# Start addresses of the SBUF slots in a fused attention and two-layer feed-forward kernel

## Chip, cores, metric

One core of a Trainium2 chip. The metric is the device time of one execution in microseconds (us). The kernel before takes 512.0 us, the median of three runs (511.82 to 512.19).

## What is computed

```python
scores = softmax(causal(q @ k.T / sqrt(64)))       # 2 batches x 12 heads, 448 tokens, head size 64
x = (scores @ v), heads side by side               # 896 tokens x 768
h = x @ w_in1;  x = (h * cos(h)) @ w_out1          # 768 -> 2048 -> 768
h = x @ w_in2
g = where(h >= 1, h, where(h <= -1, 0, (h + 1)**2 / 4))
out = g @ w_out2                                   # 2048 -> 768
```

The weights arrive as 64-bit floats.

## The kernel before

**Stages.** Attention comes first. Its last matmuls give way to ten groups of six products (`FILL`, line 599) of the first feed-forward layer. Then come the rest of that layer (`stage_in_plain`, line 854), its output layer (`stage_out(0)`, line 1009), the second input layer (`stage_in_split`, lines 1274 and 1369) and the second output layer (`stage_out(1)`, line 1009 again). The layers use two-level Strassen-like sums, so that one product serves several blocks.

**The matmuls that matter here.** From line 599 to the end TensorE runs 2106 matmuls of one shape: a 128x128 block of weights against 128x448 elements of the token side, both `fp32r` (4 bytes). Every value is split in a high and a low part, so each block product is three matmuls: weight high times token high, weight high times token low, weight low times token high. Each matmul is preceded by its own load of the weights (`LDWEIGHTS`), and the load for the next matmul runs while the current one streams its tokens.

**Slots.** Weights lie in four slots, `w0` to `w3`, each 128 partitions x 6144 bytes, used in rotation (`sw` in `stage_out` takes `w{t % 4}`). Token-side operands lie in slots of 7168 bytes: `x0` to `x5` hold the attention's output, then in `stage_out` the split halves `sx` (a ring of `x0`, `x1`, `x2`), then in the second input layer the pieces `rx` (slots `x0` to `x9`, `x14`) and `re` (slot `e0`) by the table `PIECES`. The first product of `stage_out(0)` is an exception: its token side `sx0.0h`, `sx0.0l` lies in `b0` and `b1`. The slots `b0` to `b6` hold raw 64-bit rows as 16-bit words (`RAW` = 3076 of them), later also sums and results.

**Addresses.** `place` gives each slot its tile. The slots in `EARLY` come from pool `x_p`, which is open from the start; all others come from `sum_p`, which is opened over the attention's pools once those are done. Slots follow each other in the order in which they are first asked for. 6152 bytes of a raw slot take up 6176, which is 24 x 256 + 32, so each raw slot moves all that follow it by 32 bytes modulo 256. A weight block (512 bytes), a half of a weight slot (3072) and the 1792 bytes of 448 tokens are whole multiples of 256, so within a slot every operand begins at the slot's own remainder.

**Order.** `Plan` sets the order of the work from line 854 on by modelled durations and fixed due times; `STEPS` sets it by hand for the attention. Neither looks at addresses.

Of the kernel before, what the change touches and what calls it, by code (L numbers as in the profile page):

```python
# [12 lines left out]
F32 = mybir.dt.float32  # L13
# [10 lines left out]
P = 128  # L24
# [5 lines left out]
U16 = mybir.dt.uint16  # L30
# [251 lines left out]
def attention_then_two_ffn(  # L282
# [23 lines left out]

    UW = KD * P
    RAW = 4 * UW + 4

    const = ctx.enter_context(tc.tile_pool(name="const", bufs=1))  # L310
    x_p = ctx.enter_context(tc.tile_pool(name="x", bufs=1))
# [14 lines left out]
    EARLY = {f"x{c}" for c in range(KD)} | {"b0", "b1", "b2", "w0", "w1", "w2", "w3"}  # L326
    pools = [x_p]

    def place(slot, name, shape, dtype):
        return pools[slot not in EARLY].tile(shape, dtype, tag=slot, name=name)  # L330

    raws, ready = {}, {}

    def fetch_unit(u, raw):
        w_in, f = (w_in1, w_in2)[u // KF], u % KF
        nc.sync.dma_start(
            out=raw[:, 1 : RAW - 3].rearrange("p (n f) -> p n f", f=4 * P),
            in_=w_in[:, f * P : (f + 1) * P].bitcast(U16).rearrange("(n p) f -> p n f", p=P),
        )

    def load_unit(u):
        raws[u] = place(f"b{u % 3}", f"raw{u}", [P, RAW], U16)
        fetch_unit(u, raws[u])
# [28 lines left out]
    def decode_unit(u):  # L372

        raw = raws[u]
        decode_top(tops[0], raw)
        yield
        decode_bits(words(raw), tops[0], raw)
        yield
        fl = words(raw).bitcast(F32)
        ready[u] = w = place(f"w{u}", f"w{u}", [P, 2, UW], F32R)  # L380
        nc.scalar.copy(out=w[:, 0], in_=fl)
        yield
        nc.vector.tensor_tensor(out=w[:, 1], in0=fl, in1=f32(w[:, 0]), op=ALU.subtract)
        load_unit(u + 3)
# [7 lines left out]
    class Pair:  # L392
# [5 lines left out]
        def load(self, _=None):  # L398
            n = self.n
            self.k = ld.tile([P, S], F32, tag="k", name=f"k{n}", bufs=6)  # L400
            nc.sync.dma_start(out=self.k, in_=k[n])
            self.qr = self.q = ld.tile([P, S], F32, tag="qr", name=f"qr{n}")
            (nc.scalar if n == 0 else nc.sync).dma_start(out=self.qr, in_=q[n])
# [174 lines left out]
    def decode(u):  # L578

        if u not in decodes:  # L580
            decodes[u] = decode_unit(u)
        run(decodes[u])
# [3 lines left out]
    def ffn_in_part(u, x, b, chunks):  # L586

        if u not in parts:
            bank = int(next(pairs_of_banks))
            parts[u] = (bank, ready[u], set())  # L590
            made.append(u)
        bank, w, done = parts[u]
        s = slice(b * S, (b + 1) * S)
        for c in chunks:
            first = not any((b, i) in done for i in range(KD))
            done.add((b, c))
            last = all((b, i) in done for i in range(KD))
            for n, (a, t) in enumerate(((0, 0), (0, 1), (1, 0))):
                nc.tensor.matmul(  # L599
                    psum[:, bank + b, :S], w[:, a, c * P : (c + 1) * P], x[c][:, t, s],  # L600
                    start=(first and n == 0), stop=(last and n == 2),
                )
# [11 lines left out]
    def one_bank():  # L614
        return psum[:, int(next(single_banks))]

    with ExitStack() as attn:
        ld = attn.enter_context(tc.tile_pool(name="ld", bufs=4))
        st = attn.enter_context(tc.tile_pool(name="st", bufs=3))
        once = attn.enter_context(tc.tile_pool(name="once", bufs=1))  # L620
        pairs = [Pair(n) for n in range(B * NP)]
        pairs[0].load()

        ones = nc.const_aps.tensor(1.0, [P, 512], BF16)
        warm = one_bank()
        for _ in range(8):
            nc.tensor.matmul(warm, ones[:, :P], ones, start=True, stop=True)
        ident = once.tile([P, P], F32, name="ident")
        make_identity(nc, ident)


        mask32 = once.tile([QB, QB], F32, name="mask32")
        make_causal_mask(nc, mask32, mask_val=MASKED)
        both = once.tile([P, 3 * HALF], BF16, name="both")
        nc.vector.memset(both, 0.0)
        above = once.tile([P, 2, 2, HALF], BF16, name="above")
        nc.vector.memset(above, MASKED)
        for h in (slice(0, HALF), slice(HALF, P)):
            nc.vector.tensor_copy(out=both[h, HALF:QB], in_=ident[h, h])
            for m in range(2):  # L640
                nc.vector.tensor_copy(out=above[h, m, 0], in_=mask32[h, h])
        upper, lower = both[:, HALF:], both[:, HALF:QB]
        for top in tops:
            nc.gpsimd.memset(top, 0)

        nc.scalar.activation(out=once.tile([P, 1], F32, name="first"), in_=half, func=AF.Exp)
        x1 = [place(f"x{c}", f"x1{c}", [P, 2, NT], F32R) for c in range(KD)]
        pairs[1].load()
        for word in STEPS.split():
            what, n = re.fullmatch(r"([A-Za-z]+)(\d+)", word).groups()  # L650
            n = int(n)
            if what == "raw":
                load_unit(n)
            elif what == "D":
                decode(n)
            elif what == "F":
                u, b, chunks = FILL[n]
                ffn_in_part(u, x1, b, chunks)
            elif what[0] == "l":
                (pairs[n].load if what == "l" else pairs[n].load_v)()  # L660
            else:
                getattr(pairs[n], what[0])(what[1:])
# [5 lines left out]
    MW = ML * P  # L668
    sum_p = ctx.enter_context(tc.tile_pool(name="sum", bufs=1))
    pools.append(sum_p)  # L670

    plan = Steps()
    things = {}

    def buf(name, slot, shape, dtype=F32, given=()):
        plan.buf(name, slot, given)
        things[name] = (slot, shape, dtype)

    def tile_of(name):
        t = things[name]  # L680
        if isinstance(t, tuple):
            t = things[name] = place(t[0], name, t[1], t[2])
        return t
# [72 lines left out]
    def load_raw(u, slot):  # L756
        name = f"raw{u}"
        buf(name, slot, [P, RAW], U16)
        load(f"L{u}", lambda: fetch_unit(u, tile_of(name)), [(name, p) for p in RAW_PARTS])
# [38 lines left out]
    def ws_buf(k, j, h):  # L798
        name = f"ws{k}.{j}.{h}"
        if name not in things:  # L800
            buf(name, WS_SLOT[k, h][j], [P, 2, 2, MW])
        return name
# [7 lines left out]
    def rows(k, n):  # L810
# [3 lines left out]
        name = f"rows{k}.{n}"  # L814
        buf(name, ROW_SLOT[k][n], [P, RAW], U16)
        ws = ws_buf(k, j, q // 2)

        def fetch():
            nc.sync.dma_start(out=tile_of(name)[:, 1 : RAW - 3], in_=w_out[f * P : (f + 1) * P, :].bitcast(U16))

# [650 lines left out]
```

## Time and profile before

| what | us |
|---|---|
| median of three runs | 512.0 |
| the profiled execution | 511.94 |
| its span, first to last instruction | 510.2 |
| TensorE busy (share of the span) | 504.0 (99%) |
| VectorE busy | 367.8 (72%) |
| ScalarE busy | 350.3 (69%) |
| GpSimd busy | 103.7 (20%) |

The page's busy time of TensorE counts overlapping matmuls as one stretch, so 99% says that it hardly idles, not how densely its matmuls follow each other. The length of one matmul in the trace (some 0.36 us) is longer than the distance from one start to the next (some 0.20 us), since matmuls are pipelined. The pace is therefore read from starts: of n matmuls that follow each other, from the first start to the next group's first start, divided by n.

### The profile page before, as it was taken

Reading aid. Unit: us, or ns where it says so; the run is one execution under the profiler, and the core shown is the slowest. Engines: PE = TensorE matmul, PEld = TensorE weight load, DVE = VectorE, ACT = ScalarE, POOL = GpSimd, SP = SyncE. Lnnn points to the kernel's source line nnn. Section 1 sums busy time; section 2 is a strip of 40 time slices with the busy share of each in tenths; the row PEclk is TensorE's granted clock in tenths of the full one; section 3 lists DMA queues with packets and bytes.
Section 4 is the critical chain, followed back from the end, with each engine's and each line's share of the span. In section 5 each row is a group of like instructions: output and inputs, shape, how many; then the busy total and the mean of one; then the engine's idle time right before and its main releaser. Section 6 shows DMA issues by size and latency. Waiting matters only on the chain.

```text
span 510.2 us, 7594 instructions
## 1 busy us (share of the span) xinstructions
PE 504.0 (99%) x2810; PEld 448.7 (88%) x2810; DVE 367.8 (72%) x502; ACT 350.3 (69%) x607; POOL 103.7 (20%) x165
## 2 busy tenths in 40 slices
PE   8999999999999999999999999999999999999997
PEld 4766678999999999999999999999999999999996
DVE  7878876587656656687668977777878699764760
ACT  5998977687656556655557778888788678656441
POOL 4847660000000113334001101111101012610000
PEclk9999999999999999999999999999999999999999
DMA  8845124778692478999226786775685869992111
GB/s 272 296 134 174 41 78 159 255 246 255 236 275 71 107 160 187 222 187 191 51 69 174 170 214 184 215 193 154 172 284 129 251 153 276 171 221 52 54 55 55
DMA packets 45861, 87.26 MB, mean 171 GB/s; under 512 B 2816, under 2 KB 33536, under 8 KB 45824
## 3 DMA queue, kind: packets, MB, share of 16 engines
q1 hardware_dynamic: 36464, 61.51, 36.5%
q0 software_dynamic: 9216, 25.04, 27.0%
q8 instruction: 22, 0.36, 0.3%
q10 hardware_dynamic: 144, 0.23, 0.1%
q14 instruction: 15, 0.12, 0.1%
HBM read 58.98 MB, written 2.75 MB: 121 GB/s over the span
## 4 chain that ended last, share of the span: by engine, by line
PE 97%; DVE 1%; DMA 1%; issue 0%; ACT 0%; POOL 0%; POOLq 0%
PE psum L1009 40%; PE psum L854 20%; PE psum L1274 15%; PE psum L1369 6%; PE psum L555 4%; PE psum L529 4%; PE psum L442 4%; PE psum L599 2%; DMA qr<-in_q 1%; PE psum L427 1%; DVE nma L466 0%; PE psum L452 0%; PE psum L455 0%; DVE nmc L466 0%; DVE raw L368 0%
## 5 line engine op out<-in xcount | busy, mean ns | idle before, releaser
L854 PE MATMUL psum<-x,w 128*128 128x448 f32 x516 | 103.7, 363 | 0.0
L854 PEld LDWEIGHTS psum<-x,w 128*128 128x128 f32 x516 | 96.8, 188 | 6.7
L368 DVE SCALAR_TENSOR_TENSOR raw<-raw,top 128x768 uint32<-128x768 uint32 x32 | 30.6, 957 | 14.7 <-ACT top L359 11.5
L359 ACT CAST top<-raw 128x768 f16<-128x768 bf16 x26 | 27.9, 1074 | 9.6 <-DMA raw<-in_moe_w_in 9.5
L529 PE MATMUL psum<-ident,p 128*128 128x128 f32 x192 | 24.8, 278 | 0.6 <-POOL p L509 0.6
L555 PE MATMUL psum<-pT,v 128*64 128x448 f32 (+3 forms) x192 | 23.2, 385 | 0.9 <-ACT pT L546 0.9
L1274 PE MATMUL psum<-rx,w1g 128*128 128x448 f32 x108 | 24.0, 366 | 0.0
L1274 PE MATMUL psum<-rx,w0g 128*128 128x448 f32 x108 | 23.8, 364 | 0.0
L1274 PE MATMUL psum<-rx,w2g 128*128 128x448 f32 x108 | 23.7, 364 | 0.0
L529 PEld LDWEIGHTS psum<-ident,p 128*128 128x128 f32 x192 | 20.6, 141 | 3.3 <-issue 0.9
L555 PEld LDWEIGHTS psum<-pT,v 128*64 128x64 f32 x192 | 12.6, 136 | 12.0 <-issue 6.4
L509 POOL TENSOR_SCALAR p<-p,ra 128x384 f32<-128x384 f32 (+1 forms) x48 | 22.2, 482 | 3.1 <-DVE rb L494 1.2
L707 POOL DMA_DIRECT2D raw<-raw x12 | 10.2, 850 | 61.1 <-DVE raw L712 48.3
L509 POOL TENSOR_SCALAR p<-p,rb 128x256 f32<-128x256 f32 (+1 forms) x32 | 18.2, 581 | 19.1 <-DVE rb L495 18.0
L1274 PEld LDWEIGHTS psum<-rx,w1g 128*128 128x128 f32 x108 | 20.3, 188 | 1.8
L1274 PEld LDWEIGHTS psum<-rx,w2g 128*128 128x128 f32 x108 | 20.3, 188 | 1.5
L1274 PEld LDWEIGHTS psum<-rx,w0g 128*128 128x128 f32 x108 | 20.3, 188 | 1.5
L442 PE MATMUL psum<-k,q 64*128 64x256 f32 (+2 forms) x132 | 20.5, 409 | 0.0
L442 PEld LDWEIGHTS psum<-k,q 64*128 64x128 f32 x132 | 12.3, 186 | 5.0 <-ACT p L487 1.3
L487 ACT ACTIVATE p<-psum,nmb 128x256 f32<-128x256 f32 x24 | 11.3, 478 | 6.9 <-DVE nmb L468 3.5
L487 ACT ACTIVATE p<-psum,nma 128x384 f32<-128x384 f32 x24 | 13.8, 583 | 1.4 <-DVE nmd L466 0.7
L727 DVE TENSOR_TENSOR w<-raw,w 128x768 fp32r<-128x768 f32 x14 | 13.3, 949 | 0.9 <-ACT w L718 0.9
(640 smaller groups left out, 1307.0 us busy)
## 6 DMA issues: line engine op xcount, KB each, us to landing
raw<-in_moe_w_in SPq DMA_DIRECT2D x32, 768.0 KB, 5.2
v<-in_v SPq DMA_DIRECT2D x12, 256.0 KB, 4.9
k<-in_k SPq DMA_DIRECT2D x12, 224.0 KB, 4.6
c<-c POOLq DMA_DIRECT2D x4, 672.0 KB, 7.4
out<-c SPq DMA_DIRECT2D x12, 224.0 KB, 1.9
qr<-in_q SPq DMA_DIRECT2D x11, 224.0 KB, 4.0
raw<-raw POOLq DMA_DIRECT2D x12, 192.0 KB, 4.4
rows0.0_1280<-in_moe_w_out SPq DMA_DIRECT2D x1, 768.0 KB, 4.2
```

The lines of the kernel that those rows point to most:

```text
L359: nc.scalar.copy(out=to, in_=what)
L368: nc.vector.scalar_tensor_tensor(out=fl, in0=bits, scalar=13, in1=top, op0=ALU.logical_shift_right, op1=ALU.bitwise_or,)
L442: nc.tensor.matmul(s[:, j, o : o + w], self.q[rows(n, j), i * QB : w], self.k[rows(n, j), :w], start=(o == 0), stop=False,)
L487: nc.scalar.activation(out=o, in_=i, func=AF.Exp, bias=nm[:, m : m + 1], scale=1.0 if n else scale, accum_out=self.r[r][:, c : c + 1],)
L509: e.tensor_scalar(out=p, in0=p, scalar1=r[:, c : c + 1], scalar2=1.0, op0=ALU.mult, op1=ALU.mult)
L529: nc.tensor.transpose(o, i, ident)
L555: nc.tensor.matmul(self.o[heads(j), c * QB : S], self.v[:, j, c, :], self.pT[:, c, j, c * QB :], start=(c == 0), stop=(c == FULL),)
L727: nc.vector.tensor_tensor(out=to(), in0=what(), in1=f32(hi()), op=ALU.subtract)
L854: nc.tensor.matmul(banks_of(f"h{f}")[:, b, :S], w[:, a, c * P : (c + 1) * P], x(t, c)[:, b * S : (b + 1) * S], start=(c == first and n == ...
L1009: nc.tensor.matmul(o, wt[:, a, i * MW + d * P : i * MW + (d + 1) * P], r[:, i], start=(p in (0, 1, 2) and j == 0 and i == 0 and n == 0), s ...
L1274: nc.tensor.matmul(o, wt[:, l, block, c * P : (c + 1) * P], rt[:, s, x], start=(n in (1, 5) and c == 0 and e == 0), stop=(c == ML - 1 and ...
L1369: nc.tensor.matmul(o, wt[:, l, block, c * P : (c + 1) * P], rt[:, s, x], start=(n == 0 and c == 0 and e == 0), stop=(n == 1 and c == ML - ...
```

## The change

A raw slot is allocated as 3200 words (6400 bytes, 25 x 256) of which the first 3076 are used as before, and two small tiles that nothing reads are put in: 96 bytes after `x5` and 160 bytes at the start of `sum_p`.

```diff
     RAW = 4 * UW + 4
+    RAW_ROOM = -(-RAW // P) * P
...
     def place(slot, name, shape, dtype):
-        return pools[slot not in EARLY].tile(shape, dtype, tag=slot, name=name)
+        pool = pools[slot not in EARLY]
+        if dtype == U16:
+            return pool.tile([P, RAW_ROOM], U16, tag=slot, name=name)[:, :RAW]
+        return pool.tile(shape, dtype, tag=slot, name=name)
...
         x1 = [place(f"x{c}", f"x1{c}", [P, 2, NT], F32R) for c in range(KD)]
+        x_p.tile([P, 24], F32, tag="gap0", name="gap0")
...
     sum_p = ctx.enter_context(tc.tile_pool(name="sum", bufs=1))
     pools.append(sum_p)
+    sum_p.tile([P, 40], F32, tag="gap1", name="gap1")
```

Start of each slot modulo 256 bytes, in the built programs:

| slot | before | after |
|---|---|---|
| `x0` to `x5` | 224 | 224 |
| `b0`, `b1`, `b2` | 224, 0, 32 | 64, 64, 64 |
| `w0` | 32 | 64 |
| `w1`, `w2`, `w3` | 64 | 64 |
| `x6`, `x14` | 96 | 224 |
| `x7` | 160 | 224 |
| `x8`, `x9`, `e0` | 192 | 224 |
| `b3`, `b4`, `b5`, `b6` | 64, 96, 128, 160 | 224 |
| other token-sized slots | 64 to 192 | 224 |
| attention's tiles | each 768 bytes further on | same remainders |

The 2106 matmuls by the remainders of their two operands (weights, tokens):

| pair | before | after |
|---|---|---|
| 64, 224 | 1356 | 2088 |
| 32, 224 | 504 | 0 |
| 64, 192 | 84 | 0 |
| 32, 96 and 64, 96 | 54 and 54 | 0 |
| 64, 160 | 36 | 0 |
| 32, 192 | 12 | 0 |
| 32, 0 | 6 | 0 |
| 64, 64 (the 18 matmuls of `sx0.0`) | 0 | 18 |

On every engine the instructions and their waits stand in the same order before and after.

## Rows read from the trace of the kernel before

**Rows 1.** Chain that ended last, in order of time: start us, us, what.
```profile
82.45 12.29 PE psum L599 x60
94.74 103.55 PE psum L854 x516
198.29 101.23 PE psum L1009 x504
299.52 74.84 PE psum L1274 x369
374.36 1.85 PE psum L1369 x9
376.21 1.80 PE psum L1274 x9
378.01 27.42 PE psum L1369 x135
405.43 101.19 PE psum L1009 x504
...
506.64 0.55 ACT c L1041
```

**Rows 2.** All waits of TensorE: engine, line, releaser, us in total, times, longest.
```profile
PE psum L555 <- ACT pT L546: 0.9, 1, 0.9
PE psum L627 <- PEq L1448: 0.8, 1, 0.8
PE psum L529 <- POOL p L509: 0.6, 1, 0.6
PE psum L442 <- DMA qr<-in_q: 0.2, 1, 0.2
PE psum L427 <- POOL q L414: 0.2, 1, 0.2
```

**Rows 3.** Timeline of TensorE, start of line 1009: start us, us, instructions, count.
```profile
198.12 0.37 PE L1009 MATMUL psum<-sx0.0h,sw0.0_1965 128*128 128x448 f32 x1
...
201.81 3.79 PE L1009 MATMUL psum<-sx0.1_2051,sw0.1_1993 128*128 128x448 f32 x18
205.44 3.76 PE L1009 MATMUL psum<-sx0.2_2060,sw0.2_2066 128*128 128x448 f32 x18
209.04 3.76 PE L1009 MATMUL psum<-sx0.3_2102,sw0.3_2089 128*128 128x448 f32 x18
212.64 3.81 PE L1009 MATMUL psum<-sx0.4_2138,sw0.4_2112 128*128 128x448 f32 x18
216.28 3.77 PE L1009 MATMUL psum<-sx0.5_2167,sw0.5_2141 128*128 128x448 f32 x18
...
227.09 3.81 PE L1009 MATMUL psum<-sx0.8_2250,sw0.8_2233 128*128 128x448 f32 x18
230.74 3.77 PE L1009 MATMUL psum<-sx0.9_2276,sw0.9_2252 128*128 128x448 f32 x18
```

**Rows 4.** Timeline of TensorE, 96.5 to 111.8 us, line 854.
```profile
96.21 15.77 PE L854 MATMUL psum<-x,w 128*128 128x448 f32 x78
```

**Rows 5.** Timeline of TensorE, second input layer, line 1274.
```profile
308.46 2.01 PE L1274 MATMUL psum<-rx,w1g 128*128 128x448 f32 x9
310.31 1.97 PE L1274 MATMUL psum<-rx,w0g 128*128 128x448 f32 x9
...
321.24 2.00 PE L1274 MATMUL psum<-rx,w1g 128*128 128x448 f32 x9
```

**Rows 6.** Timeline of TensorE, two short windows of line 1369.
```profile
384.94 3.36 PE L1369 MATMUL psum<-rx,w2g 128*128 128x448 f32 x16
...
399.73 3.47 PE L1369 MATMUL psum<-rx,w2g 128*128 128x448 f32 x16
```

**Rows 7.** Timeline of TensorE, first matmuls of line 599, 82 to 84 us.
```profile
82.38 1.87 PE L599 MATMUL psum<-x,w 128*128 128x448 f32 x8
```

**Rows 8.** Timeline of all engines near 345 us: the weights w3g and their first use.
```profile
344.15 0.55 DVE L727 TENSOR_TENSOR w3g<-raw,w3g 128x384 fp32r<-128x384 f32 x1
...
344.95 0.98 PE L1274 MATMUL psum<-rx,w3g 128*128 128x448 f32 x4
```

**Rows 9.** Windows: PE, PEld, DVE, ACT, POOL busy us (count), PEclk, DMA share, GB/s.
```profile
298.40:375.00 76.60, 76.60 (x379) 70.89 (x378) 61.33 (x82) 61.50 (x88) 9.36 (x11) 1.00 0.73 201
```

**Rows 10.** Line 368 on VectorE, all raw slots: ns min/median/max, first and last start.
```profile
L368 DVE SCALAR_TENSOR_TENSOR raw<-raw,top x32: 946/958/1023, 27.6 to 383.6; 128x768 uint32<-128x768 uint32 x32
```

## The prediction, made before the changed kernel ran

> **What bounds the kernel now.** I read the chain that ended last first. From 82.45 us to the end it is TensorE alone, eight rows that follow each other without a gap [rows 1]; behind the last one stand only the last result's copy and its store. The waits of TensorE come next: there are five, all in attention lines or before the first matmul [rows 2], so in the 2106 matmuls from line 599 on nothing keeps TensorE waiting for data. The granted clock is 1.00 in the stretch that I take as an example [rows 9], so throttling has no part in it either. What is left is the distance from one matmul's start to the next.
>
> The eight rows add up to 424.17 us for 60 + 516 + 504 + 369 + 9 + 9 + 135 + 504 = 2106 matmuls, 201.4 ns each. They are not equal: line 854 runs at 103.55 / 516 = 200.7 ns, line 1009 at 101.23 / 504 = 200.9, line 1274 at 74.84 / 369 = 202.8, the long row of line 1369 at 27.42 / 135 = 203.1 [rows 1]. All these matmuls have one shape, so something else sets the difference, and the timeline shows that it goes with the slots:
>
> - Weights at 64, tokens at 224: `sx0.2` starts at 205.44, `sx0.3` at 209.04, `sx0.4` at 212.64, that is 3.60 us for 18, 200.0 ns each [rows 3]. In line 854, 78 matmuls of this pair: (15.77 - 0.36) / 77 = 200.1 ns [rows 4].
> - Weights at 32, tokens at 224: `sx0.4` and `sx0.8` have their weights in `w0`. 212.64 to 216.28 is 3.64 us, 202.2 ns each, and 227.09 to 230.74 is 3.65 [rows 3]. The token slot turns every three products and the weight slot every four, and the slow products are those of `w0`, whichever token slot they meet.
> - Tokens at 96, 160: nine matmuls of `w1g` with `rx6` and `rx7` take 308.46 to 310.31, 1.85 us, 205.6 ns each [rows 5].
>
> **The change, part by part.** It adds no instruction and no wait, and the order on each engine is the same. It moves addresses: 2088 of the 2106 matmuls get the pair 64, 224; the other 18, the product of `sx0.0` at the start of line 1009, get 64, 64.
>
> *Token-side and weight slots.* I take 200.0 ns for each of the 2088, as measured for this pair over 36 [rows 3] and 78 [rows 4] matmuls. For the 18 the trace has no row: the pair 64, 64 does not occur with this operand type. The nearest row is the same product at its present addresses (32 with 224 and 0): 198.12 to 201.81, 3.69 us, 205.0 ns each [rows 3]. The bounds are 200.0 ns (nothing lost) and the slowest pace above, 206; I keep 205, since 64, 64 is no pair that was seen to run well, so the 18 cost 0.09 us more than at 200. The difference between the ends is 0.1 us.
>
> *The sum.* 2106 x 200.0 = 421.20; the rows hold 424.17, so 2.97 us lie above it. Not all of it can go. The first matmuls of line 599 start up: eight of them take 1.87 - 0.36 = 1.51 us from first start to last start instead of 7 x 0.20 = 1.40 [rows 7], and that 0.11 stays. The last row of the chain counts its last matmul at its full 0.36 us instead of 0.20, 0.16 us, and that stays too. The 18 keep 0.09. 2.97 - 0.11 - 0.16 - 0.09 = 2.61. By stage, at 200.0: line 599 and 854 some 0.44, the first line 1009 0.34, lines 1274 and 1369 together about 1.5, the last line 1009 0.2. The profiled execution took 511.94 (span 510.2, 1.74 outside it); 511.94 - 2.61 = 509.33. It is 0.06 below the median of the three runs, which is nothing here: **509.3 us**, 0.5% faster.
>
> *The producers.* TensorE reaches each operand earlier, so the cover of its producers shrinks. The tightest place that I found is `w3g` in the second input layer: VectorE ends its low half at 344.15 + 0.55 = 344.70, the first matmul of the slot starts at 344.95, and the one that reads the low half is the third, at about 345.35 [rows 8], 0.65 us of cover. A group of 63 matmuls lasts 321.24 - 308.46 = 12.78 us now [rows 5] and 12.60 at 200.0, so TensorE gains 0.18 us a group. Most of what feeds a group hangs on results that TensorE itself gave in the group before, so it moves along with it; VectorE is busy for 61.33 of 76.60 us there and ScalarE for 61.50 [rows 9], about 80%, so both can follow. I count no wait. If nothing moved along, six groups would gain 1.1 us against 0.65 of cover and 0.45 us would be given back.
>
> *The other engines.* Their operands move too. Line 368 runs over all seven raw slots, with seven different remainders, and lies between 946 and 1023 ns with a median of 958 [rows 10]; 32 such instructions off the chain cost nothing either way. The attention's own tiles keep their remainders, so I change nothing there. The raw transfers and the two added tiles have no consumer on the chain; their price on the path is nothing as long as TensorE waits for nothing, which is the paragraph before.
>
> **Against the forecast: the same pair has two paces.** Two windows of line 1369 read the same instructions of two neighbouring groups, both with weights at 64 (`w2`) and tokens at 224. In one, 16 matmuls take (3.36 - 0.36) / 15 = 200.0 ns each; in the other (3.47 - 0.37) / 15 = 206.7 ns [rows 6]. Both hold for the whole stretch. So the addresses alone do not give 200: it also counts how the stretch is entered. At present the entry is renewed all the time. Every product with `w0` ends one stretch, and what comes after it settles at 200 (`sx0.5` takes 216.28 to 219.89, 3.61 us, and then stays at 3.60 [rows 3]); the slow stretch of [rows 6] was entered from another pair, 64, 96. After the change there is one entry from the attention, as now, and one more after the 18 matmuls of `sx0.0`. What that second entry gives holds for 2106 - 576 - 18 = 1512 matmuls, as nothing interrupts them.
>
> **The rivals.**
>
> *The slow pace after `sx0.0`.* Mechanism: 18 matmuls with the pair 64, 64 leave loads and streams in a relation that settles at 206.7 ns. Price: 1512 x 6.7 ns = 10.1 us, so 509.3 + 10.1 = **519.4 us**, 1.5% slower than before. It decides from the point where the slow pace lasts for more than 2.61 / 0.0067 = 390 matmuls. For it: one of the two windows of [rows 6] is in this state, entered from a pair other than 32, 224, and 64, 64 is no pair whose exit the trace shows. Against it: line 599's entry and every entry from `w0` settled at 200. Chance 0.28.
>
> *The slow pace from the first entry.* The relation at 82.4 us depends on the end of the attention. 576 x 6.7 = 3.9 us, 513.2, if `sx0.0` mends it, and 523.3 if not. The code and remainders up to there are those of before, where it settled at once [rows 4, 7]. Chance 0.07, mostly 513.2.
>
> *The addresses don't matter.* Then the difference between `w0` and its neighbours would have another cause, such as its place in the rotation, and stay: 511.9. Against it: rotations of three and of four tell token slot and weight slot apart [rows 3], and line 1274 is slow where the tokens lie at 96 and 160. Chance 0.05. The Trainium skill, "SBUF — State Buffer", section "Who interferes with whom", speaks for this case: it gives TensorE two independent read ports, one for the moving operand and one for the weights, and says that "PE and ACT never wait on anyone", so that start addresses should make no difference and the time would stay. The trace does not agree: 200.0 against 202.2 ns with the weights 32 bytes off [rows 3], 205.6 with other token slots [rows 5].
>
> *A producer comes late.* The 0.45 us above, or a stop that makes TensorE enter a stretch anew: 509.8 to 511. Chance 0.05.
>
> **How the numbers follow.** My forecast of 509.3 has a chance of 0.55; its own range is 508.9 (the 18 at 200 and the start-up gone, and the 0.2 by which runs differ) to 509.8. With the late producer that is 0.60 for faster by over 0.2% (about what a measurement of this kernel can tell from no change; below 511.0). No effect gives 0.05, and 0.01 of mixed cases, 0.06 for the same. The two slow cases, 0.28 and most of 0.07, give 0.34 for slower. Without the slow pace the range would hold 0.65, which is too little, so it has to reach to 519.4 and the 0.3 us by which that sum may be off: 508.9 to 519.7. It is two narrow places with little between them, not a broad one.
>
> **What would show it.** Right: in the chain, line 854 at 103.2 us, the first line 1009 at 100.8 to 100.9, line 1274 at 73.8 for 369, line 1369 at 27.0 for 135, and in the timeline 3.60 us from one product of line 1009 to the next, `w0` or not. The slow pace: 3.72 us from one product to the next after `sx0.0`, everywhere. No effect: `w0` products still at 3.64. A late producer: a wait of TensorE behind line 599. Wrong altogether I would be if TensorE ran below 200 ns, or if the attention changed its length, of which nothing in this trace speaks.

## The result and the profile after

The changed kernel takes 519.36 us (median of 4 runs, 519.06 to 519.49) against 511.91 us before (4 runs, 511.59 to 512.19). The ratio is 1.0145 with a 95% interval of 1.0127 to 1.0162, so it is 1.5% slower. The forecast was 509.3; the time is that of the first rival, 519.4, which had a chance of 0.28. Some executions of several kernels below take 1.3 to 2 us longer than the others of the same kernel, at a mean granted clock of 0.995 to 0.997; the profiles of the third and fourth experiment are such ones (0.98 up to 82 us, in the attention, and 1.00 behind it), so only their rows behind the attention are compared with those of others.

Where the time is, the chain that ended last tells (start us, us, what; the changed kernel, from the first product of the feed-forward layers to the end). Lines stand 4 to 6 higher than before: 603 is the former 599, 860 the former 854, 1015 the former 1009, 1280 the former 1274, 1375 the former 1369.

```profile
82.55 12.21 PE psum L603 x60
94.75 103.20 PE psum L860 x516
197.95 104.09 PE psum L1015 x504
302.04 76.26 PE psum L1280 x369
378.30 1.86 PE psum L1375 x9
380.16 1.86 PE psum L1280 x9
382.02 27.90 PE psum L1375 x135
409.92 104.17 PE psum L1015 x504
```

Set beside [rows 1], the first two rows became faster: 12.29 to 12.21 and 103.55 to 103.20, which is 103.20 / 516 = 200.0 ns a matmul. From line 1015 on every row is slower, by 2.86, 1.42, 0.01, 0.06, 0.48 and 2.98 us. All differences add up to +7.38 us; the profiled executions differ by 519.36 - 511.94 = 7.42. So all but 0.04 us of the loss lies in these eight rows, and in those behind 197.95 us.

The waits of TensorE in the changed kernel (engine, line, releaser, us in total, times, longest) are again five short ones in the attention and ahead of it, as in [rows 2], and none behind line 603:

```profile
PE psum L559 <- ACT pT L550: 0.9, 1, 0.9
PE psum L631 <- PEq L1454: 0.8, 1, 0.8
PE psum L446 <- ACT p L491: 0.5, 1, 0.5
PE psum L533 <- POOL p L513: 0.3, 1, 0.3
PE psum L446 <- DMA qr<-in_q: 0.3, 1, 0.3
```

The granted clock is as before: 0.999 over the span. It is the pace of matmuls that wait for nothing and run at the full clock. The timeline of TensorE at the start of line 1015 (changed kernel; start us, us, instructions, count) shows where it changes, and answers to [rows 3]:

```profile
197.79 0.37 PE L1015 MATMUL psum<-sx0.0h,sw0.0_1967 128*128 128x448 f32 x1
...
201.44 3.88 PE L1015 MATMUL psum<-sx0.1_2053,sw0.1_1995 128*128 128x448 f32 x18
205.16 3.88 PE L1015 MATMUL psum<-sx0.2_2062,sw0.2_2068 128*128 128x448 f32 x18
208.88 3.88 PE L1015 MATMUL psum<-sx0.3_2104,sw0.3_2091 128*128 128x448 f32 x18
212.60 3.88 PE L1015 MATMUL psum<-sx0.4_2140,sw0.4_2114 128*128 128x448 f32 x18
216.32 3.88 PE L1015 MATMUL psum<-sx0.5_2169,sw0.5_2143 128*128 128x448 f32 x18
```

The 18 matmuls of `sx0.0`, the only ones at 64, 64, take 197.79 to 201.44, 3.65 us or 203 ns each. From `sx0.1` on the pair is 64, 224, which ran at 200.0 before line 1015, and each product takes 3.72 us, 206.7 ns a matmul. By the recorded starts the distances behind `sx0.0` go 209, 207 and then 206, 207, 207 ns over and over, 620 ns for three instead of 600, for all 1512 matmuls to the end. `w0` or not makes no difference any more: `sx0.4` lasts as long as `sx0.3`.

### The profile page after: what moved, and what is told of

It reads as the page before. It is cut to its first block, busy times and chain, and to the rows that moved or that the text cites. A ratio compares the mean times of both kernels' runs of the same rounds, so it can differ in the third digit from the quotient of the medians.

```text
span 517.6 us, 7594 instructions
## 1 busy us (share of the span) xinstructions
PE 511.3 (99%) x2810; PEld 449.8 (87%) x2810; DVE 367.6 (71%) x502; ACT 350.2 (68%) x607; POOL 103.3 (20%) x165
## 3 DMA queue, kind: packets, MB, share of 16 engines
HBM read 58.98 MB, written 2.75 MB: 119 GB/s over the span
## 4 chain that ended last, share of the span: by engine, by line
PE 97%; DVE 1%; DMA 1%; issue 0%; ACT 0%; POOL 0%; POOLq 0%
PE psum L1015 40%; PE psum L860 20%; PE psum L1280 15%; PE psum L1375 6%; PE psum L559 4%; PE psum L533 4%; PE psum L446 4%; PE psum L603 2%; DMA qr<-in_q 1%; PE psum L431 1%; DVE nma L470 0%; PE psum L456 0%; PE psum L459 0%; DVE nmc L470 0%; DVE raw L372 0%
```

## The experiments

Two theories were set against each other. **Entry:** the pair 64, 224 has two paces, 200.0 and 206.7 ns; the matmuls ahead of a stretch choose one, and it stays until a product with another pair interrupts. **Place:** the output layers are slow at the new addresses by themselves, because of a place further up in the memory or of what runs beside them there. The kernel before took 512.12 us (median of 26 runs) on the chip of the first four kernels, 512.21 (one run) on that of the four map kernels, and 511.73 (11 runs) on that of the last three.

### The first product at 224 too

```diff
+        if name in FIRST_RIGHT:          # sx0.0h, sx0.0l
+            room = pool.tile([P, 40 + 2 * S], F32R, tag=slot, name=name)
+            return room[:, 40:].rearrange("p (i s) -> p i s", i=2)
         return pool.tile(shape, dtype, tag=slot, name=name)
```

> The changed kernel with one thing different: the token side of the first product of stage_out(0), sx0.0h and sx0.0l, begins 160 bytes into its slots b0 and b1, at 224 modulo 256 like all others. All 2106 matmuls then have the pair 64, 224. Theory 'entry' (the pair 64, 224 has a fast pace of 200.0 ns and a slow one of 206.7, and the 18 matmuls at 64, 64 tip it into the slow one): no tipping, 200.0 ns to the end, 509.2 to 509.3 us. Rival 'place' (the later stages are slow by their own new addresses, say by a bit above the 256 bytes): 206.7 ns from sx0.1 on as in the changed kernel, 519.3 us.

Measured: 509.53 us (6 runs, 508.65 to 510.88), ratio 0.9946 (0.9925 to 0.9967). The chain of this kernel (start us, us, what):

```profile
82.23 12.21 PE psum L607 x60
94.43 103.20 PE psum L864 x516
197.63 100.80 PE psum L1019 x504
298.44 73.80 PE psum L1284 x369
372.23 1.80 PE psum L1379 x9
374.03 1.80 PE psum L1284 x9
375.83 27.00 PE psum L1379 x135
402.83 100.81 PE psum L1019 x504
```

Every row is at 200.0 ns, but for some 0.2 us at the start of the first. The only difference from the changed kernel is the address that 18 matmuls read; the six rows from there on differ by 3.29 + 2.46 + 0.06 + 0.06 + 0.90 + 3.36 = 10.13 us, of which the 18 themselves are 0.05 and the 1512 behind them the rest. The place theory falls: the same 1512 matmuls at the same addresses run at either pace.

### One product at 32 ends the slow pace

The changed kernel, with the weights of `sx0.4` alone at 32.

```diff
+        if name == "sw0.4":
+            room = pool.tile([P, 56 + 2 * UW], F32R, tag=slot, name=name)
+            return room[:, 56:].rearrange("p (t m) -> p t m", t=2)
+        if slot == "w0":                 # the same room for all of w0
+            room = pool.tile([P, 64 + 2 * UW], F32R, tag=slot, name=name)
+            ...
```

> The changed kernel, sx0.0 at 64 as there, and one later product, number 4 of stage_out(0) (72 matmuls after the start of line 1015), with its weights at 32 instead of 64. In the kernel before, every product with weights at 32 was followed by 200.0 ns. Entry: slow for the 54 matmuls between (0.36 us), some 202 ns for the 18 at 32, then 200.0 to the end: 509.8 us. Place: 206.7 ns goes on after product 4: 519.2 us.

Measured: 509.27 us (7 runs, 509.02 to 511.35), ratio 0.9944 (0.9926 to 0.9962). The timeline of TensorE in line 1021 of this kernel (start us, us, instructions, count):

```profile
204.57 3.88 PE L1021 MATMUL psum<-sx0.2_2062,sw0.2_2068 128*128 128x448 f32 x18
208.29 3.88 PE L1021 MATMUL psum<-sx0.3_2104,sw0.3_2091 128*128 128x448 f32 x18
212.00 3.80 PE L1021 MATMUL psum<-sx0.4_2140,sw0.4_2114 128*128 128x448 f32 x18
215.64 3.76 PE L1021 MATMUL psum<-sx0.5_2169,sw0.5_2143 128*128 128x448 f32 x18
219.24 3.76 PE L1021 MATMUL psum<-sx0.6_2198,sw0.6_2171 128*128 128x448 f32 x18
```

Up to `sx0.4` a product takes 3.72 us, `sx0.4` itself 3.64, and from `sx0.5` on 3.60. All that follows stays at 200.0 ns (the later rows of the chain are 73.80, 27.00 and 100.81 us). One product with another pair, 18 matmuls, takes the stretch out of the slow pace. In the kernel before, matmuls at 32, 224 stood 27 times ahead of nine or more at 64, 224, and by the recorded starts 200.0 ns followed each time.

### The pair 64, 64 at a later place

The kernel of the first experiment, with the first product of the second output layer (`sx1.0`) at 64, 64.

```diff
+        if slot == "x0" and dtype == F32R:
+            o = 24 if name == "sx1.0" else 0
+            room = pool.tile([P, 64 + 4 * S], F32R, tag=slot, name=name)[:, o : o + 4 * S]
+            ...
```

> As e1_first_at_224, but the first product of the last stage, sx1.0 of stage_out(1), has its token side at 64: the same 18 matmuls at 64, 64, now 1602 matmuls after line 603's first instead of 576. Entry: 200.0 ns up to there, then 206.7 for the last 486: 3.2 us, 509.3 + 0.1 + 3.2 = 512.6 us; 509.4 if this exit happens to fall into the fast pace. Place: 519 us, as the stages in between stay slow.

Measured: 512.40 us (10 runs, 511.93 to 514.23), ratio 1.0007 (0.9993 to 1.0022). Two rows of its chain, the last of line 1385 and the last line 1025, and then the timeline at the joint (start us, us, what or instructions):

```profile
377.76 27.00 PE psum L1385 x135
404.76 104.10 PE psum L1025 x504
```

```profile
404.60 3.81 PE L1025 MATMUL psum<-sx1.0_3531,sw1.0_3666 128*128 128x448 f32 x18
408.24 3.88 PE L1025 MATMUL psum<-sx1.1_3696,sw1.1_3558 128*128 128x448 f32 x18
411.96 3.88 PE L1025 MATMUL psum<-sx1.2_3698,sw1.2_3738 128*128 128x448 f32 x18
```

The first 1602 matmuls run at 200.0 and the last 486 at 206.7, switched by the 18 in between. The last row is 104.10 - 100.81 = 3.29 us longer than in the first experiment; 486 x 6.7 ns = 3.26, and the 18 themselves take 0.05 more. The price goes with the count of matmuls behind the switch, whatever layer it stands in.

### `w0` back at 32

The changed kernel with `w0` where it was: 224 bytes ahead of it, 32 behind.

```diff
+        if slot == "w0" and "gaps" not in raws:
+            raws["gaps"] = pool.tile([P, 56], F32, tag="gap2", name="gap2")
+            tile_ = pool.tile(shape, dtype, tag=slot, name=name)
+            pool.tile([P, 8], F32, tag="gap3", name="gap3")
+            return tile_
```

> The changed kernel with weight slot w0 back at 32 (all other slots as changed, sx0.0 at 64): every product of w0 is entered and left through 32. Entry: w0's 576 matmuls at some 202.3 ns, all others back at 200.0 after each of them, at most 54 slow ones behind sx0.0: 509.3 + 576 x 2.3 ns = 510.6, with the slow ones up to 511.0 us. Place: three quarters of the matmuls from sx0.1 on stay at 206.7, 517 us or more.

Measured: 510.94 us (10 runs, 510.45 to 512.84), ratio 0.9981 (0.9966 to 0.9996). Three rows of its chain, the first output layer, the second input layer and the last output layer, and then the timeline around its first product (start us, us, what or instructions):

```profile
200.13 101.23 PE psum L1020 x504
301.37 74.20 PE psum L1285 x369
...
406.37 101.19 PE psum L1020 x504
```

```profile
199.97 0.36 PE L1020 MATMUL psum<-sx0.0h,sw0.0_1969 128*128 128x448 f32 x1
...
203.68 3.77 PE L1020 MATMUL psum<-sx0.1_2055,sw0.1_1997 128*128 128x448 f32 x18
207.29 3.76 PE L1020 MATMUL psum<-sx0.2_2064,sw0.2_2070 128*128 128x448 f32 x18
```

The output layers cost again what they cost in [rows 1] (101.23 and 101.19), the products between those of `w0` run at 200.0, and no stretch is slow. The expectation overlooked one thing: the weights of `sx0.0` lie in `w0` too, so its 18 matmuls are at 32, 64 here and not at 64, 64. They take 203.68 - 199.97 = 3.71 us, 206 ns each, and the pace behind them is 200.0 at once (`sx0.1` takes 3.61 us). So this kernel shows that 32, 64 leaves the fast pace and that 32, 224 keeps it, but not a way out of the slow one; only the second experiment shows that. Of the 2.97 us above 200.0 ns that the prediction counted, the addresses other than that of `w0` give back about 1.2 (512.12 - 510.94), and `w0`, once the entry is right, the rest (510.94 - 509.53 = 1.4).

### A map of pairs

Four kernels put the slots of the output layers at other multiples of 32 bytes, on top of the first experiment, and two at steps of 4 and 8 bytes, one execution of each.

```diff
+    WEIGHT_AT = {'w0': 48, 'w1': 0, 'w2': 16, 'w3': 32}   # words, added to 64 bytes
+    TOKEN_AT = {'x0': 8, 'x1': 16, 'x2': 24}              # words, added to 224 bytes
...
+        if slot in WEIGHT_AT and dtype == F32R:
+            o = WEIGHT_AT[slot] if name.startswith("sw") else 0
+            room = pool.tile([P, 64 + 2 * UW], F32R, tag=slot, name=name)[:, o : o + 2 * UW]
+            ...
```

> A map of pairs. As e1_first_at_224, but in the two output layers the weight slots w0 to w3 begin at 0, 64, 128, 192 and the token slots x0 to x2 at 0, 32, 64: twelve pairs, each for 18 matmuls at a time. Theory 'difference': the pace depends on weights minus tokens modulo 256 alone, so the pairs with the difference of 64, 224 (96) show 200.0 or 206.7 ns and those of 32, 96 (192) 200 on average; here 192, 0 would run at 200. Rival 'both': pairs of the same difference differ. Either way the twelve lie between 197 and 207 ns, 203.5 on average: 1008 x 3.5 = 3.5 us above e1, some 512.8 us (510 to 515), plus up to 3.5 us if lines 1274 and 1369 are entered into the slow pace.

> As p1_pairs with the token slots x0 to x2 at 96, 128, 160. Difference: 0, 160 and 64, 224 alike (96), 64, 128 and 96's pair with difference 192 at 200 on average; both: no such order. 512.8 us (510 to 515), plus up to 3.5 if lines 1274 and 1369 are entered into the slow pace.

> As p1_pairs with the token slots x0 to x2 at 192, 224, 96. Difference: 192, 96 and 64, 224 alike (96); 128, 192 and 0, 64 (192) at 200 on average; both: no such order. 512.8 us (510 to 515), plus up to 3.5 if lines 1274 and 1369 are entered into the slow pace.

> As p1_pairs with the weight slots at 32, 96, 160, 224 and the token slots at 96, 224, 32. Difference: 160, 224 and 32, 96 alike (192) at 200 on average, 96, 32 and 32, 224 alike (64) at 202.3; both: no such order. Known pairs are repeated as a control: 32, 224 at 202.3 and 32, 96 at 200. 512.8 us (510 to 515), plus up to 3.5 if lines 1274 and 1369 are entered into the slow pace.

Measured: 512.65, 512.35, 516.85 and 515.84 us. From the recorded starts, for each stretch of 18 matmuls or more with one pair in all six kernels, the mean of nine distances at its end (pairs with both slots at multiples of 32; the difference is weights minus tokens, modulo 256):

| difference | pairs | stretches | ns from start to start |
|---|---|---|---|
| 0 | 7 | 26 | 202.7 to 203.1, or 206.7 |
| 32 | 4 | 20 | 203.2 to 204.4 |
| 64 | 7 | 25 | 202.2 |
| 96 | 5 | 36 | 199.9 to 200.1, or 206.7 |
| 128 | 7 | 27 | 203.1 to 205.0 |
| 160 | 4 | 17 | 205.0 to 205.7 |
| 192 | 7 | 30 | 199.9 to 200.0 |
| 224 | 4 | 19 | 200.0, 204.4, or 206.7 to 206.8 |

Where there is one pace, it goes with the difference and not with either remainder: seven pairs at 64 all give 202.2, and seven at 192 all 199.9 to 200.0; in the rows of 32, 128 and 160 the values spread by 0.7 to 1.9 ns. Where there are two paces, the difference does not say which one comes. The pair 64, 96 ran at 200.0 four times of four behind 0, 160 and at 206.7 five times of five behind 0, 224, so here the matmuls ahead chose. But 192, 96 was slow in 7 of 7 and 96, 0 in 5 of 5, each behind two different pairs, so that the remainders may count as well at 96 is not excluded. Nor is the pair directly ahead the whole of it: behind 0, 192 the pair 64, 224 was fast four times and slow once. The pair of the change has the difference 96, one of those with two paces (64, 224 at 200.0 in 13 stretches and 206.7 in 4). The pace at 32, 224 in [rows 3], 202.2, is the value of difference 64. At 192 none of the 30 stretches has a second pace.

The joint to line 1298, where the pair becomes 64, 224 for 522 matmuls, gives three slow and three fast entries over the six kernels. The timelines of the third and the first kernel show one of each (start us, us, instructions, count):

```profile
300.75 2.01 PE L1298 MATMUL psum<-rx,w0g 128*128 128x448 f32 x9
302.60 2.02 PE L1298 MATMUL psum<-rx,w2g 128*128 128x448 f32 x9
```

```profile
300.38 1.98 PE L1298 MATMUL psum<-rx,w0g 128*128 128x448 f32 x9
302.19 1.96 PE L1298 MATMUL psum<-rx,w2g 128*128 128x448 f32 x9
```

Nine matmuls take 302.60 - 300.75 = 1.85 us in the one and 1.81 in the other, with the same instructions and one pair; the products ahead had the pairs 192, 96 and 192, 64.

> The map again, in steps of 4 and 8 bytes near the difference 192: weight slots at 192, 196, 200, 208 and token slots at 0, 8, 16 in the output layers, differences 176 to 208. If 200.0 is a floor of the whole neighbourhood: 200 to 203, 510 us. If a finer place does better: below 200 in some of the twelve; each ns on 1008 matmuls is 1 us, 508 us at the best.

> As p5_near_192 near the difference 96: weight slots at 96, 100, 104, 112 and token slots at 0, 8, 16, differences 80 to 112. The two paces of 96 (200.0 and 206.7) may lie anywhere in it: 510 to 516 us; below 200 in some of the twelve if a finer place does better.

Measured: 512.56 and 518.03 us, the first above the 510 expected with 200.0 as a floor around 192, the second above its range of 510 to 516. No pair ran steadily below 200.0 ns. Off the grid of 32 bytes the difference no longer decides: 192 gives 200.0 for the pair 192, 0, but 206.2 for 200, 8 and 206.7 for 208, 16; the pair 200, 0 runs at 200.0, and the worst, 100, 16, at 216.

### Tokens at 128, difference 192

What the map asks for: the changed kernel with two other gaps and one more, token slots at 128 in place of 224, `sx0.0` left at 64, 64.

```diff
+        x_p.tile([P, 40], F32, tag="gap2", name="gap2")
         x1 = [place(f"x{c}", f"x1{c}", [P, 2, NT], F32R) for c in range(KD)]
-        x_p.tile([P, 24], F32, tag="gap0", name="gap0")
+        x_p.tile([P, 48], F32, tag="gap0", name="gap0")
...
-    sum_p.tile([P, 40], F32, tag="gap1", name="gap1")
+    sum_p.tile([P, 16], F32, tag="gap1", name="gap1")
```

> The changed kernel with its token-sized slots at 128 instead of 224 (gaps of 160, 192 and 64 bytes before x0, after x5 and at the start of sum_p); weights at 64, sx0.0 at 64 as in the changed kernel, so the same 18 matmuls at 64, 64 stand in the way. Theory 'difference and entry': the pace hangs on weights minus tokens; 192 ran at 200.0 ns on average in every stretch of the map and had no second pace, so here nothing can tip: 200.0 to the end, 509.3 us. Rival 'any disturbance tips it': slow from sx0.1 on, 519 us.

Measured: 509.12 us (6 runs, 508.96 to 509.34), ratio 0.9937 (0.9919 to 0.9955), faster than the kernel before and than the changed one. Its timeline across the same 18 matmuls (start us, us, instructions, count), and four rows of its chain:

```profile
197.52 0.36 PE L1016 MATMUL psum<-sx0.0h,sw0.0_1968 128*128 128x448 f32 x1
...
201.17 3.76 PE L1016 MATMUL psum<-sx0.1_2054,sw0.1_1996 128*128 128x448 f32 x18
204.77 3.76 PE L1016 MATMUL psum<-sx0.2_2063,sw0.2_2069 128*128 128x448 f32 x18
208.37 3.76 PE L1016 MATMUL psum<-sx0.3_2105,sw0.3_2092 128*128 128x448 f32 x18
```

```profile
94.48 103.20 PE psum L861 x516
197.68 100.85 PE psum L1016 x504
298.53 73.80 PE psum L1281 x369
...
402.93 100.82 PE psum L1016 x504
```

The disturbance is there, 201.17 - 197.52 = 3.65 us as in the changed kernel, but behind it a product takes 3.60 us again. The distances go 197, 202, 201 ns, 200.0 on the mean, for all that follows. The disturbance costs its own 0.05 us and nothing more.

## Why the prediction went wrong

**What bounds the kernel: right.** TensorE's own pace sets the time, no wait of data does. Eight rows hold nearly the whole difference between before and after (7.38 of 7.42 us), and the first experiment gets the forecast's gain by addresses alone.

**2088 matmuls at 200.0 ns: the term that failed.** The passage "I take 200.0 ns for each of the 2088" held for 576 of them, the ones ahead of `sx0.0`: line 860 at 103.20 us is the number of the prediction. The 1512 behind it ran at 206.7 ns, 10.1 us more. As a pace that the pair can have, 200.0 was right. With the entry mended the other rows follow: 100.80, 73.80, 27.00 and 100.81.

**The rest of the sum: right in total, with slips inside.** By its own rows lines 599 and 854 lie 12.29 + 103.55 - 576 x 0.2 = 0.64 us above 200.0 ns, less 0.11 for the start that is 0.53, where the prediction writes 0.44. Of the terms that were to stay, the start kept 12.21 - 12.00 = 0.21 instead of 0.11 in the first experiment, and the last row 0.01 instead of 0.16. The eight rows of that experiment add up to 421.42, 2.75 us below the 424.17 of before, where the sum gives 2.70 with the 18 at 200.0 too. The medians differ by 512.12 - 509.53 = 2.59; the interval of the ratio allows 1.7 to 3.8 us, so that this lies near 2.61 says little.

**The 18 at 64, 64: right in size.** 203 ns each where the prediction took 205, inside its bounds. Their own price was the smallest term of the sum; what they left behind them cost 10.1 us.

**The choice between the forecast and the first rival: why the term failed.** The passage "Against the forecast" had the mechanism, the place, the count (1512) and the price (10.1 us; 10.13 between the changed kernel and the first experiment). What failed was the weight: "Against it: line 599's entry and every entry from `w0` settled at 200. Chance 0.28." Those entries from `w0` are 27 by the recorded starts, but of one pair, 32, 224, so they are one piece of evidence and not 27. Across the runs that pair leads to 200.0 every time (27 before, 35 with `w0` at 32, 1 with one product at 32). They say nothing of another pair. What the trace of before holds of other pairs ahead of a longer stretch at 64, 224 is two entries, both from 64, 96: one fast and one slow, the two windows of [rows 6]. The prediction named only the slow one as entered from such a pair. Shorter stretches say more: six matmuls of `w3g` at 64, 224 follow matmuls at 64, 192 five times (the four of [rows 8] from 344.95 us on are the start of one), and by the recorded starts their distances go 202, 203, 206, 207, 207, 206 ns each time, into the slow pace and not to 200; behind 32, 224 they go 208, 203, 201, 200. Read rightly, of the two pairs other than 32, 224 that stood ahead of six or more, one led to the slow pace each time and one every other time. 64, 64 was another such pair, and the forecast was not the likeliest case. In the runs, 64, 64 led to the slow pace three times of three (the change, and the second and third experiment).

**The slow pace from the first entry: did not come.** Lines 603 and 860 run at 200.0 in the changed kernel.

**The addresses don't matter: refuted.** The rule of the Trainium skill, "SBUF — State Buffer", section "Who interferes with whom", that TensorE's two read ports are independent and that it never waits on anyone, would, read as the prediction read it, make every row of the table equal. The table goes from 199.9 to 206.8 ns with one shape and no wait, so the traces do not agree with that reading.

**A producer comes late: did not come.** No wait of TensorE stands behind line 603 in the changed kernel, nor behind line 607, its like, in the first experiment, where the second input layer runs at 200.0 throughout; the cover of `w3g` did not run out.

**The range** of 508.9 to 519.7 held the time, because it reached for the second place; the forecast itself stood at the other end.

## What to carry to other kernels

- Where matmuls of one shape follow each other without waits, read the distance from start to start by operand slot; if it differs, look at the difference of the two operands' start addresses modulo 256 bytes. For this shape (weights 128 x 128, 448 columns, four-byte operands) a difference of 192 on a grid of 32 bytes ran at 200.0 ns in all 30 stretches of the map and in the last experiment.
- A change that makes a long loop uniform also takes away what renewed its state; ask of the one irregular piece that is left not what it costs but what it leaves behind, and take a setting without a second state over one that is equally fast in its good state.
- Many occurrences of one case count once: when the change meets a case that the trace never shows, the evidence is the nearest other cases, however few.

## What the runs showed of the hardware

- The pace of back-to-back matmuls depends on where their operands start: 200.0 to 206.8 ns on multiples of 32 bytes, up to 216 ns off them (weights at 100, tokens at 16), at a granted clock of 0.999 or more over those runs.
- One pair of addresses can have two paces, 200.0 and 206.7 ns. Between the changed kernel and the first experiment only the 18 matmuls ahead differed, and the slow pace held for 1512 matmuls, some 312 us, until the end; 18 matmuls of another pair can start it or end it.
- What in the chip keeps that state was not settled. Nor did a rule come out for which pairs lead 64, 224 into the slow pace: 64, 64 did three times of three, 64, 192 five times of five (in stretches of six), 64, 96 once in two, 0, 192 once in five, 32, 224 never in 63, 32, 64 not in its one case.
